# A planned attention + MLP kernel: the planner's own choice of the next operation is replaced by a fixed table of operation numbers

## The chip, the cores and the metric

The kernel runs on one core of a Trainium2 chip. The engines of that core work side by side: TensorE (PE in the profile; PEld are its weight loads), VectorE (DVE), ScalarE (ACT), GpSimd (POOL) and SyncE (SP), which in this kernel issues every transfer between HBM and the on-chip memory, and within it. The metric is the device time of one execution in microseconds. The kernel before takes 414.59 us (median of three runs, 414.57 to 415.31).

## The reference

Sequence length S = 2048, model width D = 512, 32 heads of width 16, a window of 8 positions with a dilation of 2, hidden width F = 1376; everything is float32. What is computed:

```python
xn  = layernorm(x)
qkv = xn @ wqkv                                   # [S, 3, 32, 16]
idx = pos[:, None] - 2 * arange(8)[None, :]       # 8 earlier positions, each second one
logits = einsum("bhsd,bhswd->bhsw", q, k[idx]) * 16 ** -0.5
logits = where(idx >= 0, logits, -1e9)
s   = einsum("bhsw,bhswd->bhsd", softmax(logits), v[idx]) @ wo
y   = layernorm(xn)
g   = silu(gelu_tanh(y @ w1 + b1) @ w2 + b2)
return x + s * g
```

## The kernel before

The sequence is laid out as 128 partitions by 16 positions, and these as two dilation halves c of eight row tiles i, 128 rows of 512 each. A float32 product is made on TensorE from fp16 numbers: each operand is split into a high and a low piece, and three products (high by high, high by low, low by high) are summed in one bank of PSUM. So `wq`, `w1`, `w2`, `wo` and the normalised rows `yT` all exist twice, and making them (scale, cast, subtract) is work of ACT, DVE and POOL at the start.

Attention runs in eight units u = (c, hb), two halves by four blocks of eight heads. In each, PE makes q, k, v of eight row tiles (L746, banks `ps` and `pl`), ACT or DVE copy them out with a scale (L759, L763), SP shifts k and v by one partition for the window's halo (L771), and DVE multiplies, reduces and sums (L805 to L863), helped by POOL (L873, L883). ACT and DVE turn the result into fp16 pieces (L846, L848), and a transposing transfer puts them into `oT` (L851). Between the units' products PE runs the MLP: four chunks ch of 512 rows by eleven column blocks f, first product L1016, second L1052; ACT applies gelu (L1033) and silu (L1068). The gate is written to a scratch tensor `gd` in HBM and read back.

At the end of each half the output projection follows. `wo_first` (half 0, in the middle of the kernel) loads gate and x, multiplies by `wo` on PE (L929), gates and adds x on DVE (L920 and its neighbours), and stores the tile (L923). `wo_last` (half 1) ends the kernel. Its rows are cut into nine parts n: tiles 0 to 6 in full width, and tile 7 as two halves of 256 columns (n = 7 and 8). For each part PE finishes the sum over the heads (L961), DVE multiplies by the gate (L993), DVE or POOL adds x (L1000, L997; POOL for n = 0, 2, 4), and SP stores it (L1002).

At the start, `center` and `direct` (L599 to L617) make the raw q, k, v of two tiles from x transposed in HBM; the other tiles go through statistics (L576), a power on POOL (`rb`, L635), the normalisation (`y0`: L661, L665 or L668) and a transpose on PE (L683) or by a transfer (L715). There are also 24 matmuls on constants (L1169, "fillers"), whose results nobody reads.

No operation is issued where it stands in the code. `Plan.add` records it with its engine, an estimated duration, a priority, the operations it must follow, and the ring buffers it uses; `Plan.issue` then emits all 1237 operations in an order that a small list scheduler chooses: for each engine it takes the ready operations that could start first by the planner's own clock, breaks near ties by priority, and takes the engine whose choice starts earliest. A ring (three `ps` banks, three `prod` buffers of 8 KB per partition, seven `f` buffers and so on) hands out the slot that by the same clock became free first. So one order of emission fixes the order on every engine, the order of the transfers on SP's queue, and which buffer each use gets; the engines then run their own lists in that order and wait for each other by semaphores.

Of the kernel before, what the change touches and what calls it, by code (L numbers as in the profile page):

```python
# [66 lines left out]
W2LATE = 6  # L67

BEFORE_W1 = (0, 1, 4, 5)

class Buf:

# [24 lines left out]
class Plan:  # L97
# [9 lines left out]
    def add(self, eng, dur, fn, reads=(), writes=(), prio=None, table=None, nbytes=0,  # L107
# [14 lines left out]
        o.n = len(self.ops)  # L122
        o.eng, o.dur, o.fn, o.table, o.nbytes = eng, dur, fn, table, nbytes
        o.port, o.rate, o.issue, o.tail = port, rate, issue, tail
        o.prio = self.prio if prio is None else prio
        o.preds, o.succs, o.bufs = set(), [], []
# [95 lines left out]
    def issue(self):  # L222
        self.start()
        engs = {o.eng: [] for o in self.ops}
        for o in self.ops:
            if not o.npred:
                engs[o.eng].append(o)
        order = []
        while len(order) < len(self.ops):
            best = None  # L230
            for e, cand in engs.items():
                lst = []
                for o in cand:
                    t = self.earliest(o)
                    ok = True
                    for b in o.bufs:
                        if b.slot is None:
                            f = min(b.ring.free)
                            if f == float("inf"):
                                ok = False  # L240
                                break
                            t = max(t, f)
                    if ok:
                        lst.append((t, o))
                if lst:
                    t0 = min(x[0] for x in lst)
                    t, o = min((x for x in lst if x[0] <= t0 + (WINDOW if x[1].prio > PURG else WURG)),
                               key=lambda x: (x[1].prio, x[1].n))
                    if best is None or (t, o.prio) < (best[0], best[1].prio):
                        best = (t, o)  # L250
            if best is None:
                raise RuntimeError("no operation can be placed")
            t, o = best
            engs[o.eng].remove(o)
            for b in o.bufs:
                if b.slot is None:
                    r = b.ring.free
                    b.slot = r.index(min(r))
                    r[b.slot] = float("inf")
            end = self.place(o, t)  # L260
            for b in o.bufs:
                b.left -= 1
                b.end = max(b.end, end)
                if not b.left:
                    b.ring.free[b.slot] = b.end
            for x in self.done(o, end, MARGIN):
                engs[x.eng].append(x)
            order.append((t, o))
        self.end = max(self.free.values())
        for t, o in order:  # L270
            o.fn()
# [1095 lines left out]
```

## Time and profile before

| what | value |
|---|---|
| median of three runs | 414.59 us (414.57 to 415.31) |
| the profiled execution | 415.18 us |
| its span in the profile | 413.4 us |
| mean granted TensorE clock | 0.999 of full |
| PE busy | 405.9 us, 98% |
| DVE busy | 379.5 us, 92% |
| ACT busy | 222.1 us, 54% |
| POOL busy | 120.3 us, 29% |
| bytes moved by the queues | 46.41 MB |

The span starts with the first recorded instruction and ends with the last; the profiled execution is 1.8 us longer than its span. PE has almost no idle time between its first and its last matmul, so what the kernel takes is nearly PE's work, plus the gaps at the start, plus what follows PE's last matmul. The views that matter are therefore the timeline of PE over the first 30 us, and those of DVE and SP over the last 15. In a timeline a row is a run of like instructions: start, length, engine, line, operation, and in brackets how long the engine sat idle before it and what released it. "SPq" rows are SP's issues of transfers; they end with the issue, not with the transfer.

### The profile page before, as it was taken

What the parts mean: (1) busy time and instruction counts of PE and PEld (TensorE: products, weight loads), DVE (VectorE), ACT (ScalarE), POOL (GpSimd) and SP (SyncE); (2) the same over time, 40 slices, a digit from 0 to 9 for tenths busy, and PEclk for the clock granted to TensorE, in tenths of its full rate; (3) what the DMA queues carried; (4) which work ended last, traced back from release to release, by engine and by line L of the source; (5) the groups of instructions that cost most, each with busy time, mean ns of one, the idle gap of its engine ahead of it and who ended that gap; (6) DMA issues with size and microseconds to landing.
All of it is one profiled execution on the core that took longest, in us unless ns stands there. A gap on an engine that the chain in (4) does not pass through costs nothing.

```text
span 413.4 us, 5554 instructions
## 1 busy us (share of the span) xinstructions
PE 405.9 (98%) x2083; PEld 206.6 (50%) x2083; DVE 379.5 (92%) x379; ACT 222.1 (54%) x353; POOL 120.3 (29%) x131
## 2 busy tenths in 40 slices
PE   8799999999999999999999999999999999999996
PEld 5555544445654455445544554455455544444443
DVE  4996989998999999989998999999999998999954
ACT  4699899994549655843384252225212393263500
POOL 3834002004380425042504330434033404520021
PEclk9999999999999999999999999999999999999999
DMA  8958717030045137720172034223604244007133
GB/s 281 397 112 258 235 61 230 0 128 1 1 142 152 28 93 183 149 46 2 48 221 75 0 102 116 68 86 88 205 7 122 88 111 145 0 18 238 23 102 131
DMA packets 47211, 46.41 MB, mean 112 GB/s; under 512 B 31785, under 2 KB 32225, under 8 KB 46673
## 3 DMA queue, kind: packets, MB, share of 16 engines
q1 hardware_dynamic: 47184, 46.06, 37.6%
q8 instruction: 16, 0.26, 0.3%
q14 instruction: 11, 0.08, 0.1%
HBM read 24.06 MB, written 7.34 MB: 76 GB/s over the span
## 4 chain that ended last, share of the span: by engine, by line
PE 92%; ACT 3%; issue 1%; DVE 1%; POOL 1%; ACTq 0%
PE z L1052 28%; PE ps L1016 28%; PE ps L746 25%; PE ps L929 5%; PE ps L961 2%; PE z L961 2%; PE pl L746 1%; ACT w L421 1%; PE pl L961 1%; ACT f L673 1%; ACT yT L687 0%; ACT wq L536 0%; POOL wq L471 0%; POOL rb L635 0%; ACT prod L661 0%
## 5 line engine op out<-in xcount | busy, mean ns | idle before, releaser
L1016 PE MATMUL ps<-yT,w 128*128 128x512 f16 (+1 forms) x528 | 120.4, 379 | 0.0
L746 PE MATMUL ps<-wq,yT 128*128 128x384 f16 x708 | 117.0, 326 | 0.2 <-DVE U L759 0.2
L1052 PE MATMUL z<-w,h 128*128 128x512 f16 x480 | 110.4, 379 | 0.0
L746 PEld LDWEIGHTS <-yT 128*128 128x128 f16 x744 | 72.5, 98 | 49.2 <-issue 1.0
L1016 PEld LDWEIGHTS <-w 128*128 128x128 f16 (+1 forms) x528 | 52.8, 100 | 61.0
L805 DVE TENSOR_TENSOR prod<-U 128x2048 f32<-128x2048 f32 x32 | 73.2, 2286 | 2.2 <-POOL prod L883 0.7
L1052 PEld LDWEIGHTS <-h 128*128 128x128 f16 x480 | 46.6, 98 | 55.5 <-issue 0.3
L808 DVE TENSOR_REDUCE L<-prod 128x128 f32<-128x2048 f32 x32 | 73.0, 2281 | 0.4
L1033 ACT ACTIVATE ps<-ps,b1T,hsc 128x512 f32<-128x512 f32 (+1 forms) x44 | 32.9, 748 | 73.4 <-PE ps L1016 72.2
L863 DVE TENSOR_TENSOR prod<-pl,U 128x2048 f32<-128x2048 f32 x28 | 63.2, 2283 | 4.2 <-POOL prod L873 4.1
L763 ACT ACTIVATE U<-ps,cs 128x384 f32<-128x384 f32 x54 | 31.2, 580 | 65.2 <-PE ps L746 65.2
L873 POOL TENSOR_TENSOR prod<-prod,prod 128x2048 f32<-128x2048 f32 x7 | 31.7, 4531 | 113.8 <-DVE prod L863 99.6
L883 POOL TENSOR_TENSOR prod<-prod 128x1024 f32<-128x1024 f32 x14 | 32.9, 2349 | 0.0
L882 POOL COPY gate<-prod 1x1 f32<-1x1 f32 x21 | 5.5, 264 | 91.0 <-DVE prod L805 82.2
L1038 DVE SCALAR_TENSOR_TENSOR h<-ps,hsc,h 128x512 f16<-128x512 f32 x40 | 29.6, 741 | 1.7 <-ACT h L1036 1.4
L1036 ACT ACTIVATE h<-ps,hsc 128x512 f16<-128x512 f32 x40 | 27.3, 684 | 1.3 <-PE z L1052 0.4
L929 PE MATMUL ps<-wo,oT 128*128 128x512 f16 x96 | 21.7, 379 | 0.0
L858 DVE TENSOR_TENSOR prod<-prod,prod 128x2048 f32<-128x2048 f32 x9 | 20.5, 2282 | 0.0
L1033 ACT ACT_TABLE_LOAD x10 | 12.8, 1283 | 8.6 <-PE ps L1016 8.5
L883 POOL TENSOR_TENSOR prod<-prod,prod 128x1024 f32<-128x1024 f32 x7 | 16.4, 2347 | 0.0
L961 PEld LDWEIGHTS <-oT 128*128 128x128 f16 x108 | 10.6, 98 | 10.4
L929 PEld LDWEIGHTS <-oT 128*128 128x128 f16 x96 | 9.4, 98 | 11.2
(179 smaller groups left out, 377.8 us busy)
## 6 DMA issues: line engine op xcount, KB each, us to landing
f<-in_A_x_dram SPq DMA_DIRECT2D x31, 256.0 KB, 3.5
U<-U SPq DMA_DIRECT2D x16, 392.0 KB, 4.0
gd<-f SPq DMA_DIRECT2D x12, 256.0 KB, 3.4
prod<-in_A_x_dram SPq DMA_DIRECT2D x8, 256.0 KB, 6.9
oT<-in_B_w_dram SPq DMA_DIRECT2D x2, 1024.0 KB
yT<-in_B_w_dram SPq DMA_DIRECT2D x2, 1024.0 KB, 7.9
f<-gd SPq DMA_DIRECT2D x8, 256.0 KB, 2.7
out_dram<-f SPq DMA_DIRECT2D x8, 256.0 KB, 2.8
```

The source lines that it names most:

```text
L746: nc.tensor.matmul(b.t[:, 0:384], y[:, s, k, o:o + P], wq[:, hb, t, k], start=(n == 0), stop=(n == 11))
L763: act(384, lambda i=i, b=b: nc.scalar.activation(U3[:, i:i + 31:15, :], b.t[:, 0:384].rearrange("p (t e) -> p t e", t=3), AF.Identity, sca ...
L805: dve(2048, lambda p2=p2, g=g: nc.vector.tensor_tensor(p2(), q, slots(Ut, KH, 2 * g), op=ALU.mult), qk + [("kh", ub, 0), ("kh", ub, 1), (" ...
L808: dve(2048, lambda pr=pr, g=g: nc.vector.tensor_reduce(L3()[:, 2 * g:2 * g + 2], pr.t.rearrange("p (r f d) -> p r f d", r=2, d=DH), AX.X, ...
L863: dve(2048, lambda: nc.vector.tensor_tensor(pr.t.rearrange("p (r f d) -> p r f d", r=2, d=DH), A3()[:, 2 * g:2 * g + 2].rearrange("p r (f ...
L873: pool(4.75, lambda: nc.gpsimd.tensor_tensor(acc.t, acc.t, p1.t, op=ALU.add), [acc, p1], [acc])
L883: nc.gpsimd.tensor_tensor(x.t[:, 0:1024], x.t[:, 0:1024], y(), op=ALU.add)
L929: nc.tensor.matmul(b.t, oT[:, hb, i // 4, s, i % 4], wo[:, t, hb], start=(hb == 0 and n == 0), stop=(hb == last and n == 2))
L961: nc.tensor.matmul(b.t[:, cols], oT[:, hb, i // 4, s, i % 4], wo[:, t, hb, cols], start=(start and hb == 0 and n == 0), stop=(stop and hb ...
L1016: nc.tensor.matmul(b.t[0:M], w1[:, s, f * 512 + k * M:f * 512 + (k + 1) * M], yT[ch][:, t, k], start=(n == 0), stop=(n == 11))
L1033: act(512, lambda: nc.scalar.activation(b.t[0:M], b.t[0:M], AF.Gelu_apprx_tanh, bias=b1T[0:M, f:f + 1], scale=hsc[0:M, 1:2]), [b, ("b1T",) ...
L1052: nc.tensor.matmul(z.t, hl[s][0:K, t * P:(t + 1) * P], w2[0:K, w, f], start=(f == 0 and n == 0), stop=(f == NF - 1 and n == 2))
```

## The change

A table `ORDER` of all 1237 operation numbers is added (64 lines of the code; line numbers of the functions behind it grow by 64 to 69). `issue` no longer chooses: it takes the operations in the table's order. The costs, priorities and margins stay in the code and no longer decide anything. The rule for the slot of a ring stays "the one with the smallest mark", but the mark that a freed slot gets is now the place in the table at which it was freed, and no longer the planned time. The operations, what each must follow, and their counts are unchanged; only their order and the slots differ.

```diff
+ORDER = (
+    0, 19, 1, 2, 110, 125, 108, 131, 114, 130, 129, 127, 109, 119, 115, 20, 124, 21, 123, 22, 112, 117, 32, 33,
...
+    1216, 1212, 1232, 1207, 1217, 1197, 1227, 1236, 911, 1202, 1222,
+)
...
-        order = []
+        order, fixed = [], [self.ops[n] for n in reversed(ORDER)]
         while len(order) < len(self.ops):
             best = None
-            for e, cand in engs.items():
+            if fixed:
+                o = fixed.pop()
+                t = max([self.earliest(o)] + [min(b.ring.free) for b in o.bufs if b.slot is None])
+                assert not o.npred and t < float("inf")
+                best = (t, o)
+            for e, cand in engs.items() if best is None else ():
...
                 if not b.left:
-                    b.ring.free[b.slot] = b.end
+                    b.ring.free[b.slot] = len(order) if ORDER else b.end
```

Of PE's 395 operations the longest run common to both orders has 170, of DVE's 335 it has 200, of ACT's 281 it has 125, of POOL's 58 it has 47, and of SP's 168 it has 91. Of 1742 uses of ring buffers, 840 get another slot. In the rows below, names are those of the program's tiles with a number (`U_86` and `U_87` are the two attention buffers, `f_96` to `f_102` the seven f buffers, `z_143` to `z_146` and `ps_139` to `ps_141` banks of PSUM), and "x2" stands for rows that repeat.

**The end of SP's list.** Before, the last transposes, then the nine stores of `wo_last` (seven whole tiles and the two halves):

```order
L983 DMA f_102<-in_A_x_dram 128x512
L983 DMA U_86<-in_A_x_dram 128x512
L851 DMA_TRANSPOSE oT<-o_105 128x8x128 x2
L1002 DMA out_dram<-U_86 128x512 x7
L1002 DMA out_dram<-U_86 128x256 x2
L1362 UNCONDITIONAL_BRANCH
```

The last store there is that of the last half tile. After the change the list ends so (L1071 is the line of `wo_last`'s stores, L992 that of `wo_first`'s):

```order
L920 DMA_TRANSPOSE oT<-o_105 128x8x128
L1052 DMA f_96<-in_A_x_dram 128x512
L1071 DMA out_dram<-U_86 128x512
L1071 DMA out_dram<-U_86 128x256
L1071 DMA out_dram<-U_86 128x512 x4
L1071 DMA out_dram<-U_86 128x256
L992 DMA out_dram<-f_97 128x512
L1071 DMA out_dram<-U_86 128x512 x2
L1431 UNCONDITIONAL_BRANCH
```

By tiles the nine stores of `wo_last` stand there as 3, first half of 7, 2, 4, 0, 6, second half of 7, then the store of tile 6 of `wo_first`, then 1 and 5. The table's last three numbers (911, 1202, 1222) are these last three stores. Before, the store of `wo_first` stood among those of its own stage.

**The end of DVE's list.** Before, it ends with the two halves of tile 7:

```order
L993 SCALAR_TENSOR_TENSOR U_86<-z_145,osc,U_86 128x512
L1000 TENSOR_TENSOR U_86<-U_86,f_102 128x512
L993 SCALAR_TENSOR_TENSOR U_86<-z_146,osc,U_86 128x256
L1000 TENSOR_TENSOR U_86<-U_86 128x256
L993 SCALAR_TENSOR_TENSOR U_86<-ps_139,osc,U_86 128x256
L1000 TENSOR_TENSOR U_86<-U_86 128x256
L1362 UNCONDITIONAL_BRANCH
```

After, both halves come earlier, and tile 6 (`z_145`) in full width is last, as it is on PE:

```order
L1062 SCALAR_TENSOR_TENSOR U_86<-z_144,osc,U_86 128x512
L1062 SCALAR_TENSOR_TENSOR U_86<-ps_139,osc,U_86 128x256
L1069 TENSOR_TENSOR U_86<-U_86 128x256 x2
L1069 TENSOR_TENSOR U_86<-U_86,f_96 128x512
L1062 SCALAR_TENSOR_TENSOR U_86<-z_145,osc,U_86 128x512
L1069 TENSOR_TENSOR U_86<-U_86,f_100 128x512
L1431 UNCONDITIONAL_BRANCH
```

So the last pair on DVE is now 512 columns wide where it was 256.

**POOL's list at the start.** Before, `rb` of the first tile is followed by the normalisation of that tile (L665) and the low piece of a quarter of `wq` (L470, L471), and the powers of the other tiles come behind it:

```order
L1106 MEMSET U_87 1x896
L635 TENSOR_TENSOR rb_151<-pb_150,halves 128x1
L665 TENSOR_SCALAR prod_94<-prod_94,mv_149,rb_151 128x512
L470 TENSOR_SCALAR prod_93<-prod_93,qsc 128x384
L471 TENSOR_TENSOR wq<-prod_93,wq 128x384
L635 TENSOR_TENSOR rb_151<-pb_150,halves 128x3
L635 TENSOR_TENSOR rb_151<-pb_150,halves 128x2
L648 TENSOR_TENSOR cT<-aa_152,halves 128x6
```

After, a clear of one row (L1175) stands between `rb` of the first tile and its normalisation, and the power of the next two tiles stands ahead of the low piece of `wq`:

```order
L704 TENSOR_TENSOR rb_151<-pb_150,halves 128x1
L1175 MEMSET U_86 1x896
L734 TENSOR_SCALAR prod_94<-prod_94,mv_149,rb_151 128x512
L704 TENSOR_TENSOR rb_151<-pb_150,halves 128x2
L539 TENSOR_SCALAR prod_93<-prod_93,qsc 128x384
L540 TENSOR_TENSOR wq<-prod_93,wq 128x384
L704 TENSOR_TENSOR rb_151<-pb_150,halves 128x3
```

Of the 24 fillers on PE, 11 instead of 15 stand ahead of the first useful matmul, and seven of those that stood in the first stretch now stand later, among the products of q, k, v and the first blocks of the MLP. On DVE the statistics of the first tile now stand ahead of the four small steps that make the scale of `wq`, and no longer behind them. In the middle of the kernel, ACT's scaling of the first unit's result (L846, then L915) now stands ahead of the last three evacuations of the third unit's q, k, v, and no longer behind all of them; ACT loads its function tables 28 times instead of 25.

58 rows, old and new, of the table ORDER are left out of this document.

## The prediction

> **What bounds the kernel now.** I read the page first, then PE's timeline at both ends, then DVE's and SP's at the end, and POOL's at the start. The page's first lines, the clock row and the chain by engine:
>
> ```profile
> span 413.4 us, 5554 instructions
> PE 405.9 (98%) x2083; PEld 206.6 (50%) x2083; DVE 379.5 (92%) x379; ACT 222.1 (54%) x353; POOL 120.3 (29%) x131
> ...
> PEclk9999999999999999999999999999999999999999
> ...
> PE 92%; ACT 3%; issue 1%; DVE 1%; POOL 1%; ACTq 0%
> ```
>
> PE is the bound. The middle shows it best; busy time in two stretches:
>
> ```profile
> 0.00:31.00 31.00, 27.29 (x146) 16.70 (x147) 24.72 (x68) 21.61 (x39) 16.28 (x24) 1.00 0.79 263
> 31.00:392.00 361.00, 360.88 (x1845) 180.90 (x1844) 343.98 (x296) 199.77 (x315) 100.24 (x104) 1.00 0.34 99
> ```
>
> The first number after a stretch's length is PE: from 31 to 392 us it is busy 360.88 of 361.00. No order can win more than 0.1 us there, since no matmul is taken away; it can only lose. What an order can move is the start, where PE waits, and the end, after PE's last matmul. PE at the start:
>
> ```profile
> 1.18 3.38 PE L1169 MATMUL z<-fours 128*128 128x256 bf16 x15 [1.18 <-DVE fours L365]
> 4.65 0.79 PE L608 MATMUL ps<-f,mean 128*128 128x128 f32 x2
> 5.24 1.06 PE L1169 MATMUL z<-fours 128*128 128x256 bf16 x4
> ...
> 6.22 1.62 PE L617 MATMUL pl<-prod,U 128*128 128x384 f32 x4
> ...
> 7.85 1.54 PE L617 MATMUL pl<-prod,U 128*128 128x384 f32 x4
> 9.22 0.49 PE L1169 MATMUL z<-fours 128*128 128x256 bf16 x3
> 9.83 1.16 PE L599 MATMUL ps<-U,mean 128*128 128x128 f32 x8
> 10.83 0.38 PE L1169 MATMUL z<-fours 128*128 128x256 bf16 x2
> 12.86 0.66 PE L683 MATMUL z<-ident,prod 128*128 128x128 f32 x4 [1.65 <-POOL prod L665]
> 13.35 2.75 PE L617 MATMUL z<-prod,U 128*128 128x384 f32 x8
> ...
> 17.84 1.85 PE L683 MATMUL z<-ident,prod 128*128 128x128 f32 x12 [0.40 <-DVE prod L668]
> ...
> 24.44 5.36 PE L746 MATMUL ps<-wq,yT 128*128 128x384 f16 x32 [0.19 <-DVE U L759]
> ```
>
> After the first useful matmul (4.65) PE has 1.65 + 0.40 + 0.19 = 2.24 us of waits and 0.38 of filler that a better order can fill: 2.6 us. Two more stretches, filled with fillers, wait for data: about 0.85 until DVE has centred the first tile (6.22), and 0.61 from 9.22 to 9.83 for the second transposed tile. With these it is 4.1, the most that PE's stream holds.
>
> The end, on DVE and then on SP:
>
> ```profile
> 407.18 0.75 DVE L993 SCALAR_TENSOR_TENSOR U<-z,osc,U 128x512 f32<-128x512 f32 x1 [1.11 <-PE z L961]
> 407.97 0.69 DVE L1000 TENSOR_TENSOR U<-U,f 128x512 f32<-128x512 f32 x1
> ...
> 409.80 0.48 DVE L993 SCALAR_TENSOR_TENSOR U<-ps,osc,U 128x256 f32<-128x256 f32 x1 [0.29 <-PE ps L961]
> 410.32 0.42 DVE L1000 TENSOR_TENSOR U<-U 128x256 f32<-128x256 f32 x1
> ```
>
> ```profile
> 341.40 2.23 SPq L972 DMA_DIRECT2D U<-gd  x4
> ...
> 372.19 3.70 SPq L983 DMA_DIRECT2D f<-in_A_x_dram  x7
> 375.94 0.43 SPq L983 DMA_DIRECT2D U<-in_A_x_dram  x1
> ...
> 399.60 11.50 SPq L1002 DMA_DIRECT2D out_dram<-U  x9
> ```
>
> PE's last matmul ends at 409.76 (408.29 + 1.47, by this row),
>
> ```profile
> 408.29 1.47 PE L961 MATMUL ps<-wo,oT 128*128 128x256 f16 x12
> ```
>
> DVE's last pair ends at 410.74, the ninth store is issued at 410.77 and ends at 411.10, and the span closes at 413.4: 2.6 us after the last issue begins. This tail is on the path to the end with nothing beside it.
>
> **The change, part by part.** *PE's work.* The same matmuls; its end moves only by what the start wins or loses, and by new waits.
>
> *DVE's last pair.* Now tile 6 in full width. From the rows, the pair of 512 columns takes 0.79 (407.18 to 407.97) + 0.69 = 1.48 us, the pair of 256 takes 0.52 + 0.42 = 0.94. So +0.54. The steps ahead of it on DVE from the last half's product on (0.48 + 0.42 + 0.42 + 0.69 = 2.0) are shorter than tile 6's own group on PE (12 matmuls of 512 columns; the row above has 1.47 for 12 of 256, so some 2.5), and DVE is free when PE ends.
>
> *SP's last issues.* The store of tile 6 must wait for DVE's very last step; behind it in SP's list stand four more issues (second half of 7, the late store of `wo_first`, tiles 1 and 5) whose data were ready before. Before, nothing stood behind it. What an issue takes next to another: eight loads from 372.19 to 375.94 are seven steps, 0.54 us each; four loads in 2.23 less one issue of 0.43 are three steps, 0.60 each. The least is the issue instruction of a store itself:
>
> ```profile
> L1002 SPq DMA_DIRECT2D out_dram<-U x9: 332/333/344, 399.6 to 410.8; - x9
> ```
>
> So 4 x 0.33 = 1.3 at best, 4 x 0.60 = 2.4 at worst; I take the loads' 0.54: +2.1, because a queue that already holds the same sizes is the nearest row.
>
> *The last store.* 256 KB, no longer 128:
>
> ```profile
> out_dram<-f SPq DMA_DIRECT2D x8, 256.0 KB, 2.8
> out_dram<-U SPq DMA_DIRECT2D x7, 256.0 KB, 2.0
> ...
> out_dram<-U SPq DMA_DIRECT2D x2, 128.0 KB, 1.7
> ```
>
> Its landing takes 2.0 where the 128 KB took 1.7: +0.3. The first row here is the bound above, 2.8 (+1.1): nine stores, 2.1 MB, now go out in some 5 us, so the last may stand behind others in the queue. That the larger store should land sooner than the smaller one is not to be expected, so the lower end is 0. The tail comes to 0.54 + 2.1 + 0.3 = **+3.0**, with ends 0.54 + 1.3 + 0 = 1.9 and 0.54 + 2.4 + 1.1 = 4.1.
>
> *The start.* DVE's and POOL's rows there:
>
> ```profile
> 8.32 0.13 DVE L441 TENSOR_SCALAR ssq<-z 128x1 f32<-128x1 f32 x1
> ...
> 8.80 0.68 DVE L576 BATCH_NORM_STATS2 bn<-prod 128x6 f32<-128x512 f32 x1
> ...
> 2.48 1.62 POOL L1106 MEMSET U<- 1x896 f32 x2
> 10.05 0.57 POOL L635 TENSOR_TENSOR rb<-pb,halves 128x1 f32<-128x1 f32 x1 [5.94 <-DVE pb L633]
> 10.73 2.08 POOL L665 TENSOR_SCALAR prod<-prod,mv,rb 128x512 f32<-128x512 f32 x1
> ```
>
> The first tile's statistics now go ahead of the scale's steps (8.32 to 8.80), which brings `rb` forward by 0.4 to 0.5, to about 9.6. But a clear of one row (1.62 for two, 0.8 each) now stands between `rb` and the normalisation, which took 10.73 to 12.81: it starts at 9.6 + 0.68 + 0.8 = 11.1 and ends at 13.2, 0.35 later than before. PE fills part of that: one of the direct products of the second tile (2.75 us for eight rows, four products of 0.69) now stands ahead of the transpose, so after the transpose three remain: 13.2 + 0.5 + 2.1 = 15.8 against 13.35 + 2.75 = 16.1 before. The second transposes wait for DVE (0.40 before); the power of tiles 1 and 2 no longer stands behind the low piece of `wq`, so they come near 15.6, and that wait goes: 0.3 + 0.4 = 0.7. Against this, seven fillers now stand among useful matmuls; about three of them meet a PE that has work, at 0.49 / 3 = 0.16 each at most: 0.4 back. I make the start a gain of **0.3**. Each of some ten handovers could be off by 0.1, so the ends are a loss of 1.0 and a gain of the full 2.6.
>
> *The middle.* At nothing, while PE's stream covers it. Its cover is thinnest where ACT's scaling of the first unit's result moves ahead of the third unit's last evacuations:
>
> ```profile
> 113.34 0.58 ACT L763 ACTIVATE U<-ps,cs 128x384 f32<-128x384 f32 x1 [1.37 <-PE ps L746]
> 115.29 0.58 ACT L763 ACTIVATE U<-ps,cs 128x384 f32<-128x384 f32 x1 [1.37 <-PE ps L746]
> ...
> 124.48 1.14 ACT L846 ACTIVATE o<-prod,osc 128x1024 f16<-128x1024 f32 x1
> ```
>
> ```profile
> 120.40 2.34 POOL L883 TENSOR_TENSOR prod<-prod,prod 128x1024 f32<-128x1024 f32 x1
> ```
>
> It waits for POOL's third sum, which ended at 122.74; three evacuations now stand behind it, and PE's next groups need their banks. In the new order DVE's product ahead of that sum comes earlier, and the sum should be ready near 112, some 1 us before it would hold PE up. If it were as late as before, the evacuation due at 115.29 would start at 122.74 + 1.14, 8.6 us late, less what three banks buffer (two steps of 115.29 - 113.34 = 1.95): 4.7 us lost. I take 0. ACT's three more table loads lie beside PE, on an engine that is busy 54%.
>
> *Sum.* 3.0 - 0.3 = +2.7: span 413.4 to 416.1, the profiled execution 415.18 to 417.9. The median stood 0.59 below that execution, so the median goes from 414.59 to **417.3 us**.
>
> **The rivals.**
> - *The start wins it back.* If the new order fills all of PE's gaps, it gains 2.6, with the data waits too 4.1: 414.59 + 3.0 - 2.6 = 415.0, or 413.5. It is faster from a gain above 3.0 on, measurably (0.2% is 0.83 us, about what a measurement here can tell from no change) from 3.8. Against it: the two data waits stand on the same loads in the same order. Chance 0.07 for the 413.5.
> - *The tail is hidden.* If the four issues pair up with DVE's last steps, or the stores' completions overlap wholly, the tail costs only DVE's 0.54, and the time is 414.59 + 0.54 - 0.3 = 414.8. Against it: a queue's list is in order, and the store of tile 6 has to wait. Chance 0.09.
> - *The clock slips.* Only 11 fillers stand ahead of 4.65 (0.225 each, done near 3.7), so PE is idle about 1 us there. The row of 15 fillers takes 0.225 us each and the later row of three 0.16, though the granted clock reads full in both. If the slow pace lasted through the eight direct matmuls (1.62 + 1.54), these would take up to 3.2 more; the filler and the wait ahead of 12.86 absorb some 1.3: +1.9, 419.2 us. Chance 0.11. [...]
> - *The middle stalls.* At ACT's early scaling or at a table load, by 1 to 2 us: 418.8. Chance 0.13.
>
> **How the numbers follow.** The forecast has 0.60; its own range is 415.5 to 418.9 (the tail's 1.9 to 4.1, the start between -1.0 and +0.2). Faster by over 0.2% (below 413.8) is the first rival, 0.07; within 0.2% the second, 0.09; slower the rest, 0.84. For 8 in 10 the range leaves out the first rival, half of the second and the far part of the stalls: 414.8 to 419.9.
>
> **What would show it.** In the profile after: PE's last matmul ends within 1 us of 409.5; DVE's last row is 512 wide; SP's last five issues begin only after it, 0.3 to 0.6 apart; the span ends about 5 us after DVE's last step instead of 2.6. The first transpose comes near 13.2, the second near 15.6. I am wrong if PE shows a new gap over 0.5 us after 31 us, if direct matmuls take twice as long, if the last issues follow faster than 0.33 apart, or if PE ends before 408.

## The result and the profile after

The changed kernel takes 420.88 us (median of four runs, 420.07 to 422.04) where the kernel before takes 414.58 beside it: 1.015 times as long, with an interval of 1.0123 to 1.0177. Four more runs of the same kernel, taken later, gave 419.85 (419.56 to 420.68) against 415.12, a ratio of 1.0117 (1.010 to 1.0134). So the change costs 4.7 to 6.3 us; 2.7 were forecast, and 420.88 lies above the forecast's range. The profiled execution took 420.07, with a span of 418.3.

The first lines of the page of the changed kernel, and the chain by engine:

```profile
span 418.3 us, 5527 instructions
PE 406.8 (97%) x2083; PEld 206.6 (49%) x2083; DVE 379.2 (91%) x379; ACT 225.8 (54%) x356; POOL 128.8 (31%) x131
...
PE 93%; DVE 4%; DMA 1%; issue 0%; ACT 0%; DVEq 0%
```

The same stretch of the middle as shown of before, busy time by engine (PE first behind the length):

```profile
31.00:392.00 361.00, 361.00 (x1851) 181.38 (x1849) 338.81 (x295) 201.33 (x314) 108.82 (x105) 1.00 0.36 97
```

In this execution PE lost nothing between 31 and 392 us. All of the span's 4.9 us went at the two ends. PE's timeline at the start:

```profile
1.18 2.53 PE L1238 MATMUL z<-fours 128*128 128x256 bf16 x11 [1.18 <-DVE fours L434]
4.54 0.80 PE L677 MATMUL ps<-f,mean 128*128 128x128 f32 x2 [0.83 <-DVE f L671]
5.13 0.64 PE L1238 MATMUL z<-fours 128*128 128x256 bf16 x2
6.12 1.65 PE L686 MATMUL pl<-prod,U 128*128 128x384 f32 x2 [0.35 <-DVE U L679]
7.56 0.63 PE L1238 MATMUL z<-fours 128*128 128x256 bf16 x2
7.99 1.49 PE L686 MATMUL pl<-prod,U 128*128 128x384 f32 x2
...
9.37 1.59 PE L686 MATMUL pl<-prod,U 128*128 128x384 f32 x4
10.79 1.05 PE L668 MATMUL ps<-U,mean 128*128 128x128 f32 x8
...
12.63 0.91 PE L686 MATMUL z<-prod,U 128*128 128x384 f32 x2 [0.56 <-DVE U L679]
13.38 0.60 PE L752 MATMUL z<-ident,prod 128*128 128x128 f32 x4
...
16.63 0.66 PE L752 MATMUL z<-ident,prod 128*128 128x128 f32 x4 [0.46 <-DVE prod L737]
```

The direct products of the first tile are the rows to look at. Before, eight of them took 1.62 + 1.54 us. Now the first four alone take 1.65 + 1.49, and only the last four run as before. They end at 10.96 instead of 9.38. The first transpose behind them, in an order of its own, is 0.5 us late, and PE's last matmul ends at 411.32 instead of 409.76, 1.56 late.

The end, on DVE and on SP, and the landings:

```profile
411.43 0.75 DVE L1062 SCALAR_TENSOR_TENSOR U<-z,osc,U 128x512 f32<-128x512 f32 x1 [0.78 <-PE z L1030]
412.21 0.69 DVE L1069 TENSOR_TENSOR U<-U,f 128x512 f32<-128x512 f32 x1
```

```profile
404.39 9.35 SPq L1071 DMA_DIRECT2D out_dram<-U  x7
413.79 0.45 SPq L992 DMA_DIRECT2D out_dram<-f  x1
414.28 0.95 SPq L1071 DMA_DIRECT2D out_dram<-U  x2
```

```profile
out_dram<-f SPq DMA_DIRECT2D x8, 256.0 KB, 2.2
out_dram<-U SPq DMA_DIRECT2D x7, 256.0 KB, 2.5
out_dram<-U SPq DMA_DIRECT2D x2, 128.0 KB, 1.9
```

DVE ends at 412.90, 1.58 behind PE's last matmul where it was 0.98. Tile 6's store is issued at 412.93, the four behind it at 413.31, 413.79, 414.28 and 414.78, and the span ends 3.5 us after the last issue begins where it was 2.6. So the stretch behind PE's last matmul is 6.98 us instead of 3.64. The two ends sum to 1.56 + 3.34 = 4.9. The changed kernel's eight executions differ by up to 2.5 us among themselves, and the profile is of one of the shorter ones; the experiments come to that.

### The profile page after: what moved, and what is told of

It reads as the page before. It is cut to its first block, busy times and chain, and to the rows that moved or that the text cites. A ratio compares the mean times of both kernels' runs of the same rounds, so it can differ in the third digit from the quotient of the medians.

```text
span 418.3 us, 5527 instructions
## 1 busy us (share of the span) xinstructions
PE 406.8 (97%) x2083; PEld 206.6 (49%) x2083; DVE 379.2 (91%) x379; ACT 225.8 (54%) x356; POOL 128.8 (31%) x131
## 4 chain that ended last, share of the span: by engine, by line
PE 93%; DVE 4%; DMA 1%; issue 0%; ACT 0%; DVEq 0%
PE z L1121 27%; PE ps L1085 27%; PE ps L815 26%; PE ps L998 5%; PE z L1030 2%; PE ps L1030 2%; PE pl L815 1%; PE pl L686 1%; DVE bn L645 1%; DMA U<-in_A_xt_dram 1%; PE pl L1030 1%; DVE yT L759 0%; DVE prod L737 0%; DVE U L679 0%; DVE f L743 0%; DVE f L671 0%
## 5 line engine op out<-in xcount | busy, mean ns | idle before, releaser
L815 PE MATMUL ps<-wq,yT 128*128 128x384 f16 x708 | 120.7, 326 | 0.8 <-DVE ssq L510 0.4
L1121 PE MATMUL z<-w,h 128*128 128x512 f16 x480 | 113.3, 379 | 0.0
L874 DVE TENSOR_TENSOR prod<-U 128x2048 f32<-128x2048 f32 x32 | 73.1, 2285 | 1.0
L942 POOL TENSOR_TENSOR prod<-prod,prod 128x2048 f32<-128x2048 f32 x7 | 40.0, 5713 | 89.9 <-DVE prod L932 73.9
L1107 DVE SCALAR_TENSOR_TENSOR h<-ps,hsc,h 128x512 f16<-128x512 f32 x40 | 29.4, 743 | 5.5 <-ACT h L1105 5.5
L915 ACT ACTIVATE o<-prod,osc 128x1024 f16<-128x1024 f32 (+1 forms) x9 | 9.4, 1050 | 15.3 <-DVE prod L927 13.3
L1030 PEld LDWEIGHTS <-oT 128*128 128x128 f16 x108 | 10.5, 98 | 10.2
```

The source lines that it names most:

```text
L815: nc.tensor.matmul(b.t[:, 0:384], y[:, s, k, o:o + P], wq[:, hb, t, k], start=(n == 0), stop=(n == 11))
L874: dve(2048, lambda p2=p2, g=g: nc.vector.tensor_tensor(p2(), q, slots(Ut, KH, 2 * g), op=ALU.mult), qk + [("kh", ub, 0), ("kh", ub, 1), (" ...
L942: pool(4.75, lambda: nc.gpsimd.tensor_tensor(acc.t, acc.t, p1.t, op=ALU.add), [acc, p1], [acc])
L1030: nc.tensor.matmul(b.t[:, cols], oT[:, hb, i // 4, s, i % 4], wo[:, t, hb, cols], start=(start and hb == 0 and n == 0), stop=(stop and hb ...
L1121: nc.tensor.matmul(z.t, hl[s][0:K, t * P:(t + 1) * P], w2[0:K, w, f], start=(f == 0 and n == 0), stop=(f == NF - 1 and n == 2))
```

## The experiments

All are the changed program with another table, so no operation is added or left out. In the diffs, F is a filler, 20 the matmul of the first transposed tile's mean, 22 to 25 its direct products, 34 and 35 two small sums for the scale of `wq`, 26 the second tile's mean, 28 to 31 its direct products, 50 the first transpose. Each set of runs has its own runs of the kernel before beside it, with a median between 414.86 and 415.12.

**The order before, through the table.**

```diff
-ORDER = (0, 19, 1, 2, 110, ...)
+ORDER = the order in which the kernel before emitted its operations
```

> The kernel before's own order, put through the table, so that only the rule for the slots of the rings differs. If the order alone makes the loss: 414.6 us, within 0.4 of before, PE ending within 0.3 us of 409.8. If slots taken in table order bring waits of their own: 415.5 to 417, with new gaps of PE or a late load.

Measured: 414.76 us against 415.02, 0.9995 (0.9986 to 1.0003). The rule for the slots of the rings costs nothing; the order makes the loss.

**The fillers back in front.**

```diff
-PE: F x11, 20, F x2, 22, F x2, 23, 34, 35, 24, 25, 26, F x2, 28 ... F x7 among later work
+PE: F x15, 20, F x4, 22, 23, 34, 35, 24, 25, F x3, 26, F x2, 28 ...
```

> The changed kernel with its 24 fillers where they stood before (15, 4, 3 and 2 in the first 13 us). Theory of the clock: the eight direct matmuls of the first tile, 0.72 to 0.75 us each for the first four now, go back to 0.39 to 0.41, they end near 9.3 instead of 10.8, and with seven fillers gone from among useful work the time falls by 1.5 to 2.5 us, to 418.4 to 419.4. Rival, that POOL and DVE in their new order hold PE up at the start: the direct matmuls may be faster but the first transpose stays near 13.4 and the time within 0.5 of 420.9.

Measured: 418.60 us, 1.0087 (1.0074 to 1.010). In its timeline of PE the direct products are back at their pace, the first transpose comes at 12.26 instead of 13.38, and the last matmul ends at 409.80, as before:

```profile
6.09 1.83 PE L686 MATMUL pl<-prod,U 128*128 128x384 f32 x4
...
7.81 1.54 PE L686 MATMUL pl<-prod,U 128*128 128x384 f32 x4
...
12.26 0.66 PE L752 MATMUL z<-ident,prod 128*128 128x128 f32 x4
```

**The converse: the changed kernel's fillers at the front of the kernel before.**

```diff
-PE: F x15, 20, F x4, 34, 22, 23, 35, 24, 25, F x3, 26, F x2, 50, 28
+PE: F x11, 20, F x2, 22, F x2, 23, 34, 35, 24, 25, 26, F x9, 50, 28
```

> The kernel before's order with the fillers of the changed one at the front (11 ahead of the first useful matmul, 2 and 2 around the first direct matmuls; the other 9 in the gap ahead of the first transpose, where PE waits anyway). Theory of the clock: the first four direct matmuls slow to 0.72 to 0.75 us each, PE ends 0.8 to 1.6 later, 415.4 to 416.3 us. Rival (fillers have no part in it): 414.6, direct matmuls at 0.39 to 0.41.

Measured: 416.48 us (416.38 to 416.88), 1.0036 (1.0024 to 1.0048), so 1.5 us more, a little above the upper end expected. Nine fillers fill the gap ahead of operation 50, where PE waits anyway (1.05 us are left of the wait), so no filler stands in PE's way; the loss is the pace:

```profile
6.15 1.65 PE L686 MATMUL pl<-prod,U 128*128 128x384 f32 x2 [0.35 <-DVE U L679]
...
8.02 1.48 PE L686 MATMUL pl<-prod,U 128*128 128x384 f32 x2
...
14.18 0.66 PE L752 MATMUL z<-ident,prod 128*128 128x128 f32 x4 [1.05 <-POOL prod L734]
```

These two runs settle what happened at the start of the changed kernel. Spacings in the traces say when the pace changes: fillers lie 0.21 us apart at the slow one, 0.11 at the full one. With 15 fillers in front the step came between 3.8 and 7.0 us in all fourteen profiles; with 11 in front it came between 8.9 and 10.2 in all six. What differs ahead of it is that PE stands idle for 0.8 us, from 3.7 to 4.5. The granted clock in the profile's rows reads 1.00 in all these stretches and does not show it: the trace's records of the clock begin only with the first grant of full speed, at 6.38 us in the kernel before and at 9.49 after the change, and the rows count the time ahead of it as full.

The busy time ahead of the step differs with it. From its first filler at 1.18 us to the first grant at 6.38 PE was busy for 5.11 of 5.20 us in the kernel before. In the changed kernel it was busy for 4.01 of the same 5.20 us, and the grant came 3.11 us later, at 9.49, with PE busy for all of those 3.11 us. From the first grant on the clock is full for 406.19 us in both traces. How much work has to go ahead of the step is not shown by these runs. (The ends of matmuls are modelled in the profile, so these times are not exact.)

The step also differs between executions. In the three profiles with the changed kernel's own start and no gap of PE behind 31 us (this kernel twice, and once with an edit near 340 us) it comes at 8.93, 9.49 and 10.20 us; PE's last matmul ends at 411.04, 411.32 and 411.68, and the executions take 419.79, 420.07 and 420.42. So a step 1.27 us later put PE's end 0.64 us later, half of the delay, and made 0.63 us of the spread of the changed kernel. How far the step can move was not shown.

**Where the seven late fillers count.** Two runs that came later; the first has the changed kernel with an edit of SP's order that is described further down (the k halos first).

```diff
-PE: F x11, 20, F x2, 22, F x2, 23, 34, 35, 24, 25, 26, F x2, 28 ... F x7 among later work
+PE: F x11, 20, F x2, 22, F x2, 23, 34, 35, 24, 25, 26, F x9, 28 ...
```

> The same with 11 fillers in front as in the changed kernel, but its seven late fillers moved into the gap ahead of the second tile's direct products. If the late fillers cost their own time in a full stream: 7 x 0.11 = 0.77 less than 420.4, 419.5 to 419.8, direct matmuls of the first tile slow as in the changed kernel. If they cost nothing: 420.4; if they cost more than their time, because each stands between a product and its evacuation: below 419.3.

Measured: 420.08 us (419.75 to 420.51) against 420.37 for the same kernel with its late fillers. That is 0.3 less, within the spread of both, and not 0.8: the direct products are as slow as in the changed kernel (1.65 + 1.49 us for the first four). That the late fillers lie partly in waits that stay is likely and not shown.

```diff
-kernel before: F x15, 20, F x4, 34, 22, 23, 35, 24, 25, F x3, 26, F x2, 50, 28 ...
+kernel before: F x15, 20, F x2, 34, 22, 23, 35, 24, 25, 26, 50, 28 ... F x7 among later work
```

> The kernel before with 15 and 2 fillers at the front and seven of its others among q, k, v products and the first blocks of the MLP, as the changed kernel has them. If each costs its 0.11 in a full stream: 0.5 to 0.9 above before, 415.4 to 415.9, direct matmuls at full pace from about 6.5. If two fillers behind the first matmul are too few to keep the clock: 1.4 more, direct matmuls slow to 9 us.

Measured: 416.32 us (416.23 to 416.83), 1.0033 (1.0021 to 1.0046), 1.5 us more and not 0.8. The profile, of the longest of the six executions, shows a thing that neither reason had in it. The first direct products run at full pace, but PE then stands idle for 1.87 us ahead of the transpose, with no filler there, and the next eight direct products are slow:

```profile
12.97 1.11 PE L752 MATMUL z<-ident,prod 128*128 128x128 f32 x4 [1.87 <-POOL prod L734]
13.88 3.94 PE L686 MATMUL z<-prod,U 128*128 128x384 f32 x8
```

3.94 us where the kernel before takes 2.75 for them. Here the clock row of the page (40 slices of the span, in tenths) shows it:

```profile
PEclk9899999999999999999999999999999999999999
```

The trace's record has half the clock from 12.88 to 16.30 us. It begins at the end of PE's idle 1.87 us; the kernel before, with its fillers, is idle for 1.65 us there and keeps the clock. So the fillers ahead of 9.8 and 12.9 us are not idle work either: without them the pace fell back in this execution. But that does not explain the median. These 3.42 us at half take 0.4% off the execution's mean granted clock, so a stretch of that length leaves at most 0.996; four of the six executions have 0.998 to 1.000 and still take 416.24 to 416.37 us. What the late fillers cost in these beyond their own 0.77 is open.

**Fifteen in front only.**

```diff
-PE: F x11, 20, F x2, 22 ... F x7 among later work
+PE: F x15, 20, F x2, 22 ... F x3 among later work
```

> The changed kernel, four of its seven late fillers moved ahead of the first useful matmul (15 there, as before), nothing else. If PE's idle 0.8 us from 3.7 to 4.5 is what costs the clock: direct matmuls at full pace from about 6.5 on (spacing 0.32 to 0.40 instead of 0.64 to 0.80 us), PE's last matmul 1.3 to 1.8 earlier, 1.7 to 2.2 less with the four late fillers' 0.11 each: 418.0 to 418.9 where the changed kernel has 419.9 to 420.9. Rival, that the number of matmuls between 4.5 and 6.1 matters (two fillers there, four before): direct matmuls stay slow to 9 us, 0.4 less only.

Measured: 420.48 us (419.62 to 421.37). The profiled execution, the one of 421.37, has its direct products at full pace and a gap of PE of 1.86 us at 348 us, which hides the effect. So it was tried again without what makes that gap:

> The same with four of the late fillers moved ahead of the first useful matmul (15 there), now without the race in the middle that hid the effect. Theory of the clock: direct matmuls at full pace from 6.6 us on, 0.9 to 1.6 us below the version with the halo alone: 418.0 to 419.0. Rival, that loads and DVE set the start anyway: 0.4 less at most, by the four fillers' own time.

Measured: 420.43 us (419.45 to 420.61) against 420.37 for the same with 11 in front. The profiled execution (419.68) has the full pace (0.91 + 0.81 us for the first four direct products), but waits for the second transposed tile:

```profile
10.02 1.16 PE L668 MATMUL ps<-U,mean 128*128 128x128 f32 x8 [0.43 <-DMA U<-in_A_xt_dram]
```

All 24 fillers in their old places, in the same setting, do gain:

> The changed kernel with the k halos first (420.4) and all 24 fillers where they stood before. If the first trial of these fillers (418.6) holds without the race: 418.3 to 418.8. If its gain was chance of the loads' arrival: 419.5 to 420.4, as with 15 in front.

Measured: 418.63 us (418.35 to 419.35), 1.7 below the version with 11 in front, which repeats the first trial. So it takes the fillers between the loads too, and 15 in front alone did not do it in the median. Three of its five executions lay near 420.5 and none of them has a profile. A fall-back as in the kernel before without its middle fillers was not the reason: their mean granted clocks are 0.997, 0.997 and 0.998, and 3.42 us at half the clock, as there, leave at most 0.996. The reason is open.

**The stores when their data are ready.**

```diff
-SP's end: stores of tiles 3, 7a, 2, 4, 0, 6, 7b, wo_first's tile 6, 1, 5
+SP: wo_first's tile 6 behind its own addition; end: 1, 3, 2, 0, 4, 7b, 7a, 5, 6
```

> The changed kernel with only the stores moved: the one of the first half behind its own addition, the nine of the end in the order in which their data come ready, so that the store of tile 6 is the last. Theory of the queue: DVE's last step unchanged near 412.9, the last issue right behind it instead of 1.85 us later, and the end 2.0 to 2.8 us earlier: 418.1 to 418.9. Rival, that the bytes in flight and not the issues set the end: 0 to 0.8 earlier, since the same bytes go out in the same last microseconds.

Measured: 418.40 us (417.23 to 419.51), 1.0078 (1.006 to 1.0096), 2.5 below the changed kernel. The last issue now stands directly behind DVE's last step, which in this execution ends at 414.77: tile 6's store begins at 414.80, and the span ends at 417.7, 2.9 later. The stretch behind PE's last matmul is 4.51 us instead of 6.98. This profile also has a gap of PE of 1.85 us near 348 us, to which the text comes below.

**The queue alone, in the kernel before.**

```diff
-SP's end: 0, 2, 1, 3, 4, 5, 6, 7a, 7b
+SP's end: 0, 2, 4, 6, 7b, 7a, 1, 3, 5
```

> The kernel before, only SP's last stores in another order: behind the store of the last half tile stand four more, of 128, 256, 256 and 256 KB, whose data are ready. Theory of the queue: the last issue begins 1.8 to 2.1 us later, the landing takes 0.3 to 0.9 more, 2.1 to 3.0 in all: 416.8 to 418.0 us. Rival, that issues are hidden by transfers: 0 to 0.5.

Measured: 417.37 us (417.21 to 418.08), 1.0056 (1.0044 to 1.0069): 2.25 more. DVE's and SP's last rows:

```profile
409.71 0.42 DVE L1069 TENSOR_TENSOR U<-U 128x256 f32<-128x256 f32 x1
```

```profile
398.99 13.46 SPq L1071 DMA_DIRECT2D out_dram<-U  x9
```

DVE ends at 410.13, the last issue ends at 412.45, and the span at 415.4. Four issues behind a store that waits, with the landing of a larger last store, cost 2.3 us in one order and 2.5 in the other.

**Both mends, and the tail of before.**

```diff
 fillers and stores as above; wo_first's store behind the halo transfers
```

> The changed kernel with both mends: fillers where they stood before, stores in the order of their data (the store of the first half behind the halo transfers and the gates, not ahead of them). If the start and the queue are separate terms they add: 420.9 - 2.3 - 2.5 = 416.1, and what is left over the kernel before is 1.5. If they share something: 417 or more. If the race of the run with the stores moved came from that one store being ahead of the halo transfers, no PE gap over 0.5 us after 31 us.

Measured: 416.59 us (416.07 to 416.89), 1.0034 (1.0021 to 1.0047). The two terms add, within 0.5 us: 420.88 - 2.3 - 2.5 = 416.1. Counted from all eight executions of the changed kernel (median 420.37) the terms are 1.8 and 2.0, and the sum is 416.6.

```diff
-PE and DVE finish: 5, 7a, 7b, 6
+PE and DVE finish: 5, 6, 7a, 7b
```

> The same, and PE and DVE finish as before: tile 6 ahead of the two halves of tile 7, whose store of 128 KB is the last. By DVE's rows 0.54 less for the last pair, and 0.3 to 0.9 less for the landing: 0.8 to 1.4 below the kernel without this edit, 414.7 to 415.3. Rival, that the last landing is set by the bytes in the queue: 0.5 less only.

Measured: 416.48 us, with seven executions from 415.94 to 416.62 and two at 418.11 and 418.37. So the narrow last pair gained 0.1 in the median and 0.2 for those seven, not 0.8 to 1.4: both forecasts missed. DVE has fallen behind here: its rows from tile 5 on (410.49 us) stand without a pause, and the last pair ends 1.65 us behind PE's last matmul, where it was 1.58 with the wide one. The profile is of 418.11 and shows where the other 1.9 went: PE stands idle for 1.86 us at 347.5 us, and one of DVE's products takes 6.54 us.

**The race in the middle.** That product is the first of the last unit (L874), and the step of POOL beside it is its sum of two buffers (L942). Each reads two operands from SBUF, the memory on the chip that holds the tiles `prod` and `U`. In the changed order the product stands directly behind the step that releases POOL's sum, and both become ready within some tenths of a microsecond, the product with the last unit's halo transfers. Two runs push it either way:

```diff
-SP: copy of one row, wo_first's tile 7, k halo x2, transpose, v halo x2
+SP: k halo x2, copy of one row, wo_first's tile 7, transpose, v halo x2
```

> The version with fillers, stores and tail mended, and on SP two small steps (a store of the first half, the copy of one row) moved behind the last unit's two halo transfers of k, which so start about 0.7 us earlier. Theory of the race between DVE's first product of that unit and POOL's sum: its slow executions (418.1 and 418.4 among nine at 415.9 to 416.6) vanish, all within 415.9 to 416.7, no PE gap near 347. Rival, that the stall has another cause: one in four or five executions still near 418.2.

```diff
-SP: copy of one row, wo_first's tile 7, k halo x2, transpose, v halo x2
+SP: copy of one row, wo_first's tile 7, v halo x2, k halo x2, transpose
```

> The version with fillers and stores mended (416.1 to 416.9 in six executions), and the last unit's two halo transfers of v put ahead of those of k, which so start about 1.4 us later. Theory of the race: POOL's sum starts first in most or all executions, DVE's 2048-wide product takes over 6 us instead of 2.28, PE shows a gap of 1 to 2 us near 347, and the time is 417.8 to 418.6. Rival: no change, 416.1 to 416.9.

Measured: with k first, 416.14 us (415.86 to 416.64 in ten executions), none above 416.7; with v first, 418.40 us (418.24 to 418.84 in five), all above 418. DVE, then POOL, with k first:

```profile
339.69 2.28 DVE L874 TENSOR_TENSOR prod<-U 128x2048 f32<-128x2048 f32 x1
```

```profile
339.92 6.45 POOL L942 TENSOR_TENSOR prod<-prod,prod 128x2048 f32<-128x2048 f32 x1 [10.43 <-DVE prod L932]
```

and with v first, where PE's timeline has the gap:

```profile
341.70 4.98 DVE L874 TENSOR_TENSOR prod<-U 128x2048 f32<-128x2048 f32 x1 [1.82 <-DMA U<-U]
```

```profile
340.02 4.51 POOL L942 TENSOR_TENSOR prod<-prod,prod 128x2048 f32<-128x2048 f32 x1 [10.44 <-DVE prod L932]
```

```profile
347.40 1.68 PE L1121 MATMUL z<-w,h 128*128 128x512 f16 x7 [1.85 <-DVE h L1107]
```

The one that starts first keeps its pace, 2.28 or 4.51 us, and the other ends about its own length behind it: POOL 4.40 us behind DVE with k first, DVE 2.15 behind POOL with v first. In the kernel before, a DVE product that takes one operand from a bank of PSUM (L863) starts 0.41 us into a POOL sum of the same size and takes its 2.28 us all the same. If DVE loses, the low piece of `h` behind it on DVE (L1107) is late, and PE waits (1.85 us).

What the best of these versions has left over the kernel before, 1.0 us at 416.14, stands for the most part on DVE: PE's last matmul ends at 409.80, against 409.76, but DVE's last pair 1.66 us behind it instead of 0.98.

Is this why the changed kernel's own runs spread?

> The changed kernel unchanged, for a second profile and more times, since its executions lay 2 us apart (420.07 to 422.04) where those of the kernel before lie within 0.8. Theory of the race: one of DVE's 2048-wide products starts just behind one of POOL's sums in some executions and takes over 4 us instead of 2.28, as in the run with the stores moved; then a slower profile shows one new gap of PE after 31 us, 0.5 to 2 us long. Rival, that the slow clock at the start lasts longer in some executions: no gap after 31 us, PE's last matmul later by what the direct matmuls lost. Second rival: only the time behind PE's last matmul differs.

> The changed kernel, with only the last unit's two halo transfers of k moved ahead of two small steps on SP. Theory of the race: the slow half of the changed kernel's executions (420.5 to 422.0) vanishes, the rest stays: 419.4 to 420.1 in all, no PE gap near 347. Rival, that its spread has another cause: executions up to 421 or 422 as before.

Measured: 419.85 us (419.56 to 420.68) for the unchanged second trial, whose profile (419.79) again has no gap behind 31 us but an earlier step of the clock, as said above; 420.37 us (420.05 to 420.67) with the k halos first. So the highest executions (421.1, 422.04) are gone, but the lowest are too, and the median did not fall. The race belongs to the order, since 421.37 with 15 fillers in front shows it with the changed kernel's own middle; how often it falls out badly in the changed kernel itself is open, and it is not what sets the median. In its two profiles DVE's product starts first, and so it does with the k halos first.

**Does any order of the start gain?**

```diff
 DVE: 54,
+37, 38,
 36,
-37, 38, 39, 44,
 68, 27,
+44, 39,
 PE:
+28,
 50,
-28,
 29, 30, 31
```

> The kernel before's order with three moves at the start and nothing else: on DVE the first tile's statistics ahead of the scale of wq, and the second tile's centring ahead of a low piece of wq; on PE one direct product of the second tile ahead of the first transpose, in the gap of 1.65 us. If PE's gap is what costs there: the first transpose about 0.3 earlier, the direct products done 0.7 to 1.0 earlier, the powers for the next tiles too (POOL's low piece waits for that product), and 413.4 to 413.9 us. Rival, that DVE or the loads set the next transposes anyway: 414.4 to 414.7.

Measured: 414.64 us against 415.12, 0.9991 (0.9982 to 0.9999), too little to tell from no change. The gap of 1.65 us ahead of the first transpose shrank to one of 0.83, ahead of the direct product that now stands there, and came back behind it:

```profile
17.74 1.94 PE L752 MATMUL z<-ident,prod 128*128 128x128 f32 x12 [0.91 <-DVE prod L737]
```

The next step brought tile 2 forward on DVE, POOL and PE to fill that:

> The kernel before's order with the better start tried before, and its next gap filled: on DVE the statistics and the normalisation of tiles 1 and 2 ahead of others, their power on POOL ahead of a low piece of wq, and the transpose of tile 2 on PE right behind the direct products. If PE's gap of 0.4 to 0.9 near 17.5 us is filled: 413.9 to 414.4 where before has 415.0 in these runs. Rival, that DVE's sum of work sets the start whatever its order: 414.6 to 415.0.

Measured: 416.68 us, 1.0043 (1.0029 to 1.0056): two gaps of 1.24 and 0.97 us at 18.3 and 19.9, for DVE's and ACT's steps that it put back. That is above both forecasts. In the kernel before DVE is busy for 14.42 of the 15 us from 11 us on, so what one tile wins there another seems to lose; no run tests that by itself. No version beats the kernel before by more than the measurement can tell.

## Why the prediction was wrong

The direction was right, the size was not: 2.7 us were forecast and 4.7 to 6.3 measured.

- **That PE has nothing to win in the middle** held: 361.00 of 361.00 us in the profile after. That it has nothing to lose was taken too easily. The place that I named as thinnest, ACT's early scaling, cost nothing, but not for the reason given: POOL's sum was ready at 116.44 us and not "near 112", and PE's stream covered that too. The weak place was DVE's product beside POOL's sum, where the edge is some tenths of a microsecond and the price 1.9 us. In the profile of before no step of DVE's takes over 2.29 us, so nothing there pointed at it. The code did: this product and POOL's sum carry the flag `port`, and the planner's clock (`earliest`) holds a flagged step back until the last flagged one has ended. With the table that rule still computes a time and no longer decides anything.
- **DVE's last pair**, forecast +0.54: measured 1.58 - 0.98 = +0.60.
- **SP's four last issues**, forecast +2.1: 414.78 - 412.93 = 1.85 us, 0.46 apart.
- **The last landing**, forecast +0.3 with 1.1 as the bound: the end lies 0.9 further behind the last issue. Together 3.34 for a forecast of 3.0, and moving the stores alone gave 2.5 in the changed kernel and 2.25 in the kernel before for the queue and the landing (2.4 forecast). This part of the mechanism was right.
- **The start** was the step that failed: "I make the start a gain of 0.3", measured a loss of 1.56 at PE's last matmul. Its sum took the durations of the direct products from the profile of before and let them stand. What happened is the rival that the clock slips, priced at +1.9 with a chance of 0.11; the direct products end 1.58 late, and the converse in the kernel before's order costs 1.5. The 3.2 us in that price take all eight products at half their pace, and no run shows that: in the changed kernel four of the eight were slow, 1.65 + 1.49 us where they took 1.62. The evidence was in the quoted rows: 0.225 us for a filler at 1.18 and 0.16 at 9.22. The granted clock that reads full in both says nothing of the first, since its records begin at 6.38 us. The first useful products came near full pace (1.62 us for four) where PE had been busy for 5.11 of the 5.20 us from 1.18 on, and the new order's four fewer fillers leave 0.8 us idle exactly there. It deserved to be the main case. The range made it worse: the start's own end was "a loss of 1.0", and the range went on with a loss of 0.2.
- **Seven late fillers**, forecast 0.4 for three of them: 0.3 in the changed kernel, within the spread. But that the early ones were missed from the gaps was not in the sum at all; in the kernel before's order moving seven costs 1.5, of which only a part is explained.
- **The rest of the start's walk**: "first transpose near 13.2" came at 13.38, but by luck. POOL's normalisation, which was to set it, ended at 12.48 (`rb` started at 9.06, not 9.6), and PE came late because of its slow products; with the pace mended the transpose comes at 12.26. The second came at 16.63 against 15.6, and at 15.43 with the fillers back, so there the walk was sound but for the pace.
- **The slots of the rings** changed nothing, as taken.

The first four executions have their median 0.8 us above the profiled one, and all eight spread over 2.5. The place of the clock's step explains 0.6 of that as measured; the race in the middle can make an execution 1.9 longer. How much each has in the longest executions is not settled, nor why 15 fillers in front alone gain nothing in the median.

## What to carry to other kernels

Matmuls on constants at the start are part of the schedule: moving some of them, or leaving PE idle for under a microsecond among them, can cost more than the moved ones take (1.5 us here, where four fillers take 0.85), so look at the pace of equal matmuls and not only at their order. An in-order queue of transfers should hold at its end only what waits for the last step; each ready store behind it cost about half a microsecond here (0.46). And where the order put a DVE product with two inputs in SBUF next to a POOL sum that reads there too, the one that started second ended 4.40 us (POOL) or 2.15 us (DVE) behind the other here, and small shifts of a transfer decided which.

## What was not expected of the hardware

The profile's granted clock read 1.00 while equal matmuls ran at half their later pace (spacings of 0.21 and 0.11 us), because its records begin with the first grant of full speed, at 6.38 us in the kernel before and at 9.49 in the changed one. By 6.38 us PE had been busy for 5.11 of the 5.20 us since 1.18 in the one and for 4.01 in the other. An idle stretch of 1.87 us, in the order of the kernel before without its middle fillers, ran into 3.42 us at half the clock, and eight direct products took 3.94 us instead of 2.75; through one of 1.65 us, in the kernel before, the clock stayed full. At the end the records fall to half 2.80 us behind PE's last matmul in the kernel before and 4.35 us behind it in the changed one. Mending PE's and DVE's order at the end gained 0.2 us instead of 0.8 to 1.4, since DVE then arrived late at the last tiles by itself.
